# Loading the first batch in two pieces through one queue, with a new written-out order for units 0 to 2, in a fused attention and feed-forward kernel

## The chip, the cores and the metric

The kernel runs on one core of a Trainium2 chip. Times are device microseconds of one execution. Before the change the kernel takes 227.11 us (median of three executions, 226.82 to 227.4). A separate execution was profiled, and all views of the profile come from it.

Engines: PE is TensorE (matmuls and transposes; its weight loads appear as PEld), DVE is VectorE, ACT is ScalarE, POOL is GpSimd, SP is SyncE. DMAs are issued from the instruction streams of SP, ACT or POOL. Only those issued by POOL may change the number type on the way (float32 in DRAM, float16 on the chip), and each issue occupies POOL itself.

## The reference: what is computed

Attention over chunks, then a feed-forward layer. Inputs are float32: q, k, v of shape (4 batches, 8 heads, 768 tokens, 64), eight memory tokens per batch and head (mem_k, mem_v), a gain vector g of 512, and two weights of 512 x 2048 and 2048 x 512.

```python
for c in range(nc):                       # chunks of 32 tokens
    k_full = concat(mem_k, k[c_start - 16 : c_end + 8])     # clipped to the sequence
    v_full = concat(mem_v, v[c_start - 16 : c_end + 8])
    a = softmax(q_c @ k_full.T / 8)
    out_c = a @ v_full
x  = out rearranged to (batch, token, 512)
xn = (x - mean) / sqrt(var + 1e-6) * g
y  = x + relu(xn @ w_ch1) @ w_ch2
```

## The kernel before

**Tiles and units.** The 4 x 768 tokens are cut into 24 tiles of 128 tokens (six per batch) and 12 units of two tiles. For a tile `t` the steps are: `qk_products` (scores on PE), `row_max` and `less_max` on DVE, `weights` (exponential on ACT), `pt_products` and `pt_copy` (the weights transposed on PE and copied to SBUF), `val_products` (weights times V on PE), `tokens` (division by the row sum and the mean, on DVE), `shift` (mean taken off, on POOL or ACT), `x_products` and `x_copy` (transposition on PE, gain on DVE), and `square`, `root_of` (the deviation). For a unit `u` there are eight `up_products` blocks with `relu_up`, and then the second layer. Unit 0 uses `down_products` for that; from unit 1 on seven block products (`down7_products`) work on sums of blocks of the weights and of the activations (`w2_sum`, `r_sum`). `store` writes a finished tile from SP.

**Getting q, k and v into place.** Scores need K and Q with the head dimension on the partitions. `load_octets` brings rows of eight tokens ("octets", 512 numbers in a row) into `raw` with POOL's casting DMA. PE transposes them against an identity, and copies from PSUM spread the columns into `KT` (by `to_stream`, in groups of 72 columns with room for memory columns) or `QD` (by `to_rows`). `turn_whole` transposes blocks of 128 columns and needs the octets rearranged first by `mix_into`; `turn` transposes blocks of 64 columns directly from the raw rows. V of batch 0 goes the same way into `VT` (which is the buffer `KT[1]`, not yet in use), and `v_products`/`v_copy` turn it back into groups of rows in `V[0]`, group `g` by group `g` (12 groups). V of later batches is loaded directly in rows by `load_v_group` (two DMAs per group), and `v_shared` and `v_mem` copy overlapping rows and memory rows from SP.

**How batch 0 starts.** The first 16 octets of K, Q and V are loaded uncast (float32) by three DMAs on SP's queue (`load_first`, issued at L636 to L638 through L180) into `xs[6..8]`. DVE casts them to `xn` (L654, L659, L680), `first_turn` transposes them (L230), and `first_stream` and `first_rows` copy them into place. Octet 16, the right border of the first piece, comes with the memory rows in four DMAs on ACT's queue (`load_mem`, L174) and is put in place by `octet_cols`. POOL's queue brings octets 16 to 47 (`load_octets(..., 16, 32, ...)`, through L105) and then octets 48 to 95.

**What sets the order.** The schedule is manual: each engine executes its instructions in the order in which the program issues them. For units 0 to 2 that order is a list written out by hand, one call per line (L636 to L1034), including the bank of PSUM that each product uses. From unit 3 on a loop with a table of steps (`plan`) issues the work; that part and everything after it are the same in both kernels. PE, ACT, DVE, POOL and SP each wait in order, so an instruction whose data is late holds everything behind it on its engine. The casting DMAs use eight completion semaphores in turn, so the ninth issue waits until the first has landed, and so on. `warm(n, bank)` issues `n` matmuls of zeros (L633), whose results nobody reads.

Of the kernel before, what the change touches and what calls it, by code (L numbers as in the profile page):

```python
# [9 lines left out]
FP16 = mybir.dt.float16  # L10
# [6 lines left out]
def kernel(  # L17
# [12 lines left out]
    nc = tc.nc  # L30
# [16 lines left out]
    memT = sb.tile([128, B * 4 + 12, 8], FP16, name="memT")  # L47
# [8 lines left out]
    MR = B * H + 3 * H  # L56
# [121 lines left out]
    def load_first(queue, x, src):  # L178

        queue.dma_start(out=xs[6 + x], in_=dram(src, 0, [[512, 16], [HS, H], [1, 512]]))  # L180

# [30 lines left out]
    def mem_ends(dst, src, engine="V"):  # L212
# [6 lines left out]
        )  # L219

    def octet_cols(dst, src, group, engine):
        copy_on(engine)(
            out=free(dst, 16 + group * BLK, [[KC, 4], [1, 8]]), in_=free(src, 0, [[8, 4], [1, 8]]),
        )

    def first_turn(x, p):

        for r in range(8):
            for par in range(2):
                nc.tensor.matmul(  # L230
                    out=p[64 * par : 64 * par + 64, 64 * r : 64 * r + 64],
                    lhsT=xn[x][:, 64 * r : 64 * r + 64],
                    rhs=free(identity, 2 * par, [[4, 32], [1, 2]]),
                    start=True, stop=True, tile_position=(0, 64 * par),
                )
        return p

    def first_stream(dst, p, q0, n, engine):
        for first, cnt, at in ((0, 2, 16), (2, 6, 40)):
            copy_on(engine)(  # L240
                out=free(dst, q0 * KC + at, [[KC, n], [BLK, 2], [8, cnt], [1, 8]]),
                in_=free(p, q0 + 4 * first, [[1, n], [32, 2], [4, cnt], [64, 8]]),
            )

    def first_rows(p, q0, n, engine):
        copy_on(engine)(
            out=free(QD[0], q0 * S, [[S, n], [8, 16], [1, 8]]),
            in_=free(p, q0, [[1, n], [4, 16], [64, 8]]),
        )
# [386 lines left out]

    load_first(nc.sync, 0, k)
    load_first(nc.sync, 1, q)  # L638
    load_first(nc.sync, 2, v)
    load_mem(nc.scalar, 0, mem_k, B * H)  # L640
    load_mem(nc.scalar, B * H, k, H, 16 * 512, HS)
    load_mem(nc.scalar, B * H + H, mem_v, H)
    load_mem(nc.scalar, B * H + 2 * H, v, H, 16 * 512, HS)
    make_identity(nc, identity)
    nc.gpsimd.memset(V[0][:, 0:4, :, 64:VW], 1.0)
    nc.gpsimd.memset(V[0][0:16, 0, :, 64:VW], 0.0)

# [494 lines left out]
```

## Time and profile before

| What | us |
|---|---|
| median of the executions shown (lowest, highest) | 227.11 (226.82, 227.4) |
| the profiled execution | 226.66 |
| its span from first to last instruction | 224.9 |
| PE busy in the span | 215.5 |
| DVE / ACT / POOL busy | 168.4 / 129.0 / 114.7 |
| first instruction of `up_products` (the first real weights) | 23.90 |
| granted TensorE clock, mean over the span | 0.985 |

The page of the profile shows one execution. "Busy" is time in which an instruction of the engine runs; PE is busy 96% of the span, and from 25 us to the last units it is almost never idle. The chain of work that ended last is read backwards from the last instruction: each piece waits for the one before it. In the slices of the span, PEclk is the clock that was granted to TensorE, in tenths of full speed. A line number names the place in the kernel, which is often a helper's.

### The profile page before, as it was taken

The page shows a single profiled execution, that of the slowest core. Times are in us where ns is not written, and L with a number is a line of the kernel's source. Part 1 is how long each engine was busy: PE and PEld are TensorE (multiplying, and loading weights), DVE is VectorE, ACT ScalarE, POOL GpSimd, SP SyncE. Part 2 cuts the span into 40 slices and gives each one's busy share as a digit, 9 for nine tenths or more (in the row PEclk, how much of TensorE's full clock was granted, in tenths as well). Part 3 has the DMA queues.
Part 4 walks back from the last instruction along what each step waited for, and adds up shares of the span by engine and source line. Part 5 has one row for each costly group of instructions (what it writes and reads, how often), then busy time and mean ns, then how long its engine had stood idle before and what let it go on. Part 6 is the DMA issues. An engine that isn't in the chain of part 4 may idle for free.

```text
span 224.9 us, 8345 instructions
## 1 busy us (share of the span) xinstructions
PE 215.5 (96%) x3609; PEld 190.7 (85%) x3609; DVE 168.4 (75%) x382; ACT 129.0 (57%) x250; POOL 114.7 (51%) x198
## 2 busy tenths in 40 slices
PE   7879999997999999999999999999999999999993
PEld 2558985797998889999999999999999899999982
DVE  0996879986988886994786996994876876747372
ACT  2697473795896288378347198198266464443310
POOL 8899752969997817967346937321121130320000
PEclk9985999999999999999999999999999999999999
DMA  6999999999786994995934985942002002011022
GB/s 149 198 175 206 214 211 203 147 129 162 68 70 102 213 154 80 128 78 110 181 39 103 123 105 101 96 79 93 3 3 93 3 3 96 0 56 40 4 93 95
DMA packets 43530, 23.66 MB, mean 105 GB/s; under 512 B 30069, under 2 KB 39477, under 8 KB 43445
## 3 DMA queue, kind: packets, MB, share of 16 engines
q0 software_dynamic: 38032, 14.09, 54.2%
q1 hardware_dynamic: 5364, 8.93, 13.7%
q8 instruction: 28, 0.46, 0.9%
q10 hardware_dynamic: 96, 0.11, 0.2%
q14 instruction: 10, 0.07, 0.1%
HBM read 29.05 MB, written 6.29 MB: 157 GB/s over the span
## 4 chain that ended last, share of the span: by engine, by line
PE 89%; DVE 4%; ACT 2%; DMA 2%; issue 0%; POOL 0%; SPq 0%; ACTq 0%
PE upb L489 32%; PE dnb L566 28%; PE two L405 4%; PE one L306 3%; PE one L489 3%; PE dnb L489 3%; PE one L354 2%; PE one L385 2%; DMA xs<-in_q_dram 2%; PE one L461 2%; PE upb L515 2%; PE one L515 2%; PE one L566 1%; PE upb L306 1%; PE dnb L328 1%; DVE nmx L363 1%
## 5 line engine op out<-in xcount | busy, mean ns | idle before, releaser
L489 PE MATMUL upb<-xT,w1c 128*128 128x256 f16 x656 | 84.7, 273 | 0.3 <-ACT rT L481 0.3
L489 PEld LDWEIGHTS <-w1c 128*128 128x128 f16 x768 | 81.3, 114 | 2.2 <-issue 0.5
L481 ACT ACTIVATE rT<-upb 128x512 f16<-128x512 f32 x81 | 47.1, 594 | 30.0 <-PE upb L489 30.0
L573 DVE SCALAR_TENSOR_TENSOR xs<-dnb,rstd,xs 128x256 f32<-128x256 f32 x73 | 35.1, 481 | 24.1 <-PE dnb L566 23.2
L566 PEld LDWEIGHTS <-RS 128*128 128x128 f16 x352 | 33.6, 98 | 3.5 <-issue 0.2
L376 ACT ACTIVATE P<-sub 128x512 f16<-128x512 f32 x24 | 15.1, 632 | 35.1 <-DVE sub L366 35.1
L566 PE MATMUL dnb<-T,RS 128*128 128x256 f16 x248 | 31.8, 273 | 0.0
L428 POOL TENSOR_SCALAR xn<-xs,nmean 128x512 f16<-128x512 f32 x20 | 14.1, 707 | 29.2 <-PE upb L489 17.5
L566 PEld LDWEIGHTS <-rT 128*128 128x128 f16 x264 | 25.2, 98 | 2.5
L448 POOL TENSOR_SCALAR veps<-ssq 128x1 f32<-128x1 f32 x24 | 4.5, 189 | 40.7 <-ACT sq L441 40.0
L560 DVE TENSOR_TENSOR RS<-rT 128x1024 f16<-128x1024 f16 (+2 forms) x23 | 15.2, 663 | 8.9 <-ACT rT L481 8.9
L566 PE MATMUL dnb<-w2c,rT 128*128 128x256 f16 x168 | 21.6, 273 | 0.0
L441 ACT ACTIVATE sq<-xs,nmean 128x512 f16<-128x512 f32 x24 | 17.2, 718 | 0.5 <-ACT sq L441 0.4
L415 DVE CUSTOM_DVE_ANT_1 xs<-two,rec 128x512 f32<-128x512 f32 x24 | 16.6, 692 | 0.8
L452 POOL TENSOR_TENSOR rstd<-veps,mhalf 128x1 f32<-128x1 f32 x24 | 13.9, 578 | 2.0
L114 POOL DMA_DIRECT2D V<-in_v_dram x16 | 13.4, 840 | 0.7 <-PE dnb L566 0.6
L363 DVE TENSOR_REDUCE nmx<-one 128x8 f32<-128x512 f32 x19 | 13.0, 685 | 1.0 <-PE one L354 1.0
L470 DVE TENSOR_TENSOR xT<-one,g_col 128x512 f16<-128x512 f16 x16 | 11.0, 687 | 3.5 <-PE one L461 3.3
L366 DVE TENSOR_TENSOR sub<-one,nmx 128x512 f32<-128x512 f32 x19 | 13.1, 691 | 0.6
L393 ACT COPY PT<-one 128x512 f16<-128x512 f16 x16 | 9.3, 584 | 4.2 <-PE one L385 3.4
L405 PEld LDWEIGHTS <-PT 64*32 64x32 f16 x768 | 7.5, 94 | 4.9 <-issue 3.7
L566 PE MATMUL dnb<-w2c,RS 128*128 128x256 f16 x88 | 11.4, 272 | 0.0
(144 smaller groups left out, 361.3 us busy)
## 6 DMA issues: line engine op xcount, KB each, us to landing
out_dram<-xs SPq DMA_DIRECT2D x23, 256.0 KB
raw<-in_k_dram POOLq DMA_DIRECT2D x14, 192.0 KB, 6.0
raw<-in_q_dram POOLq DMA_DIRECT2D x14, 192.0 KB, 6.3
w1c<-in_moe_w_ch_dram POOLq DMA_DIRECT2D x4, 512.0 KB, 11.5
w2c<-in_moe_w_ch_dram POOLq DMA_DIRECT2D x4, 512.0 KB, 16.0
V<-in_v_dram POOLq DMA_DIRECT2D x16, 77.0 KB, 3.8
V<-memv SPq DMA_DIRECT2D x6, 120.0 KB
V<-V SPq DMA_DIRECT2D x2, 360.0 KB
```

Source lines behind the costliest of these rows:

```text
L363: nc.vector.tensor_reduce(out=nmx[t % 2], in_=scores, axis=AX.X, op=ALU.max)
L376: nc.scalar.activation(out=P[t % 3], in_=sub[t % 2], func=ACTF.Exp, scale=0.125)
L405: nc.tensor.matmul(out=two[col : col + 32, 128 * h : 128 * h + 65], lhsT=PT[t % 3][rows, 2 * (h // 4) + h % 2, q0 : q0 + 32], rhs=V[b % 2] ...
L415: nc.vector.tensor_tensor_reduce(out=x.rearrange("p (h d) -> p h d", h=H), in0=free(two, 0, [[128, 8], [1, 64]]), in1=free(r, 0, [[1, 8], ...
L428: nc.gpsimd.tensor_scalar(out=xn[i], in0=x, scalar1=m, scalar2=1.0, op0=ALU.add, op1=ALU.mult,)
L441: nc.scalar.activation(out=sq, in_=xs[t % 9], func=ACTF.Square, bias=nmean[t % 6], scale=1.0, accum_out=ssq[i],)
L452: nc.gpsimd.tensor_tensor(out=rstd[t % 9], in0=veps[i], in1=mhalf, op=ALU.pow)
L481: nc.scalar.activation(out=o, in_=i, func=ACTF.Relu)
L489: nc.tensor.matmul(out=p[:, 256 * hb : 256 * hb + 256], lhsT=free(w1c[hc // 4][:, dt, :], hc % 4, [[4, 128]]), rhs=xT[u % 3][:, dt, :], st ...
L560: nc.vector.tensor_tensor(out=RS[k][:, lo:hi, :], in0=a[:, lo:hi, :], in1=b[:, lo:hi, :], op=op)
L566: nc.tensor.matmul(out=p[:, 0:256], lhsT=left[:, n, :], rhs=right(n), start=(n == 0 and not add), stop=(n == 7), skip_group_check=add,)
L573: nc.vector.scalar_tensor_tensor(out=x, in0=p[:, 0:256], scalar=rstd[t % 9], in1=x, op0=ALU.mult, op1=ALU.add,)
```

## The change

Batch 0 is loaded only by POOL's casting queue, in a different cut: octets 0 to 47 of K and V, octets 0 to 31 of Q, then octets 32 to 95 of Q and 48 to 95 of K and V. The three uncast loads, the three casts, `first_turn`, `first_stream`, `first_rows`, `octet_cols` and the two DMAs for octet 16 are gone. K and Q of the first piece are transposed by `turn` straight from the raw rows, V by `mix_into` and `turn_whole`. The memory rows (40 instead of 56) come by two DMAs on SP's queue; the gain vector `g_col` is loaded right behind them instead of at 8.9 us. The cast of the memory rows moves from DVE to ACT, the first columns of ones in V are set by DVE instead of POOL, and `make_identity` comes on POOL behind the first three loads. The list for units 0 to 2 is another one: the same tiles and units, with other orders, banks and engines for the copies. Some of it, with the list cut where it only reorders:

```diff
-    memT = sb.tile([128, B * 4 + 12, 8], FP16, name="memT")
+    memT = sb.tile([128, B * 4 + 4, 8], FP16, name="memT")
-    MR = B * H + 3 * H
+    MR = B * H + H
-    def load_first(queue, x, src):
-        queue.dma_start(out=xs[6 + x], in_=dram(src, 0, [[512, 16], [HS, H], [1, 512]]))
-    load_first(nc.sync, 0, k)
-    load_first(nc.sync, 1, q)
-    load_first(nc.sync, 2, v)
-    load_mem(nc.scalar, 0, mem_k, B * H)
-    load_mem(nc.scalar, B * H, k, H, 16 * 512, HS)
-    load_mem(nc.scalar, B * H + H, mem_v, H)
-    load_mem(nc.scalar, B * H + 2 * H, v, H, 16 * 512, HS)
-    make_identity(nc, identity)
+    load_mem(nc.sync, 0, mem_k, B * H)
+    load_mem(nc.sync, B * H, mem_v, H)
+    nc.sync.dma_start(out=g_col, in_=dram(moe_g_ln, 0, [[1, 128], [128, 4]]))
-    warm(9, upb[0])
-    copy_on("V")(out=xn[1], in_=xs[7])
-    load_octets(0, 0, k, 0, 16, 32, (0,))
-    load_octets(0, 0, k, 0, 16, 32, (1,))
-    warm(2, one[0])
-    fq = first_turn(1, one[0])
...
+    warm(7, upb[0])
+    load_octets(0, 0, k, 0, 0, 48, (0,))
+    load_octets(0, 0, k, 0, 0, 48, (1,))
+    load_octets(1, 0, q, 0, 0, 32, (1,))
+    copy_on("A")(out=mem16, in_=mem32)
+    make_identity(nc, identity)
+    mem_products(one[0])
+    mem_copy(one[0], "V")
+    mem_cols(KT[0], memT[:, 0:4, :], "V")
+    mem_ends(KT[0], memT[:, 0:4, :], "A")
+    load_octets(1, 0, q, 0, 0, 32, (0,))
+    warm(6, one[1])
+    tk0 = turn(raw[0][0], 0, 48, one[1])
+    load_octets(2, 0, v, 0, 0, 48, (0,))
+    mem_cols(VT, memT[:, 16:20, :], "V")
+    load_octets(2, 0, v, 0, 0, 48, (1,))
+    to_stream(KT[0], tk0, 0, "V", 48, 0)
+    load_octets(1, 1, q, 0, 32, 64, (0,))
+    tk1 = turn(raw[0][0], 1, 48, upb[0])
+    to_stream(KT[0], tk1, 1, "V", 48, 0)
+    load_octets(1, 1, q, 0, 32, 64, (1,))
+    load_octets(0, 1, k, 0, 48, 48, (1,))
+    warm(1, upb[1])
+    tq1 = turn(raw[1][0], 1, 32, upb[1])
+    to_rows(0, tq1, 1, "V", 32, 0, 0, 16)
+    mix_into(whole[0], raw[2][0], 0, 96, "V")
+    load_octets(2, 1, v, 0, 48, 48, (0,))
+    load_octets(2, 1, v, 0, 48, 48, (1,))
+    tq0 = turn(raw[1][0], 0, 32, dnb[0])
+    load_octets(0, 1, k, 0, 48, 48, (0,))
+    to_rows(0, tq0, 0, "A", 32, 0, 0, 16)
+    warm(4, dnb[1])
+    s0 = qk_products(0, dnb[1])
+    tv0 = turn_whole(whole[0], 0, 96, one[0])
+    to_stream(VT, tv0, 0, "V", 48, 0)
+    load_w1(0)
+    mix_into(whole[0], raw[2][0], 1, 96, "A")
...
+    tv1 = turn_whole(whole[0], 1, 96, one[1])
+    to_stream(VT, tv1, 1, "A", 48, 0)
+    s1 = qk_products(1, upb[0])
+    row_max(1, s1)
+    warm(2, dnb[0])
+    v2 = v_products(2, dnb[0])
+    load_octets(1, 0, q, 1, 0, 48, (0,))
+    load_v_group(1, 11, 1)
+    load_w1(3)
+    v1 = v_products(1, upb[1])
+    load_w1(1)
+    mix_into(whole[3], raw[1][1], 1, 128, "A")
+    v0 = v_products(0, one[0])
+    v_copy(0, v0, "A")
+    row_max(0, s0)
+    v_copy(1, v1, "A")
+    less_max(0, s0)
+    weights(0)
+    load_octets(1, 0, q, 1, 0, 48, (1,))
+    less_max(1, s1)
...
+    load_w2(0)
+    to_rows(0, tQ1, 1, "A", 64, 32)
...
+    load_w1(2)
...
+    shift(1, "P")
+    shift(0, "A")
+    to_stream(KT[0], tK1, 1, "A", 48, 48)
+    load_w2(1)
+    warm(1, upb[1])
+    x0 = x_products(0, upb[1])
...
+    s2 = qk_products(2, dnb[1])
+    v_copy(5, v5, "V")
+    up_products(0, 1, upb[1])
...
+    shift(4, "P")
...
+    load_v_group(1, 3, 0)
...
+    v_shared(1, 0, 4)
...
+    v_mem(1)
...
+    val_products(6)
```

The list still issues 24 loads into `raw` and the weights' eight loads on POOL's queue, in another order and, for batch 0, in other sizes. `warm` issues 21 matmuls in all instead of 17. The second batch's first two Q loads stand ahead of most of the weights.

## The prediction

> **What bounds the kernel now.** I read the page's busy shares and slices first, then the chain of waits, then stages between chosen times, then the DMA issues.
>
> ```profile
> PE 215.5 (96%) x3609; PEld 190.7 (85%) x3609; DVE 168.4 (75%) x382; ACT 129.0 (57%) x250; POOL 114.7 (51%) x198
> PE   7879999997999999999999999999999999999993
> PEclk9985999999999999999999999999999999999999
> DMA  6999999999786994995934985942002002011022
> ```
>
> PE is the bound from the fourth slice (5.6 us each) on. So a change at the start counts in two ways only: when PE can begin the weights' stream, and how often PE idles afterwards. The first slices also show a cut clock. The stages (length, then busy time per engine with instructions, granted clock, DMA share, GB/s):
>
> ```profile
> 5.00:8.50 3.50, 2.73 (x56) 1.40 (x54) 2.62 (x12) 1.08 (x3) 2.75 (x5) 1.00 1.17 208
> 12.00:15.00 3.00, 2.34 (x89) 1.63 (x85) 2.82 (x7) 2.76 (x8) 2.94 (x5) 1.00 1.19 170
> 15.00:21.80 6.80, 6.13 (x110) 5.12 (x96) 4.59 (x16) 5.56 (x11) 6.41 (x11) 0.50 1.23 198
> 25.00:50.00 25.00, 25.00 (x454) 20.06 (x453) 22.41 (x50) 16.67 (x34) 14.84 (x26) 1.00 1.23 181
> 50.00:55.00 5.00, 3.80 (x96) 3.37 (x95) 2.82 (x5) 3.18 (x6) 4.94 (x8) 1.00 1.18 181
> 70.00:75.00 5.00, 4.70 (x51) 4.34 (x49) 4.37 (x9) 2.43 (x5) 4.67 (x10) 1.00 0.86 179
> 75.00:92.00 17.00, 16.79 (x296) 15.35 (x295) 13.33 (x33) 11.65 (x21) 10.17 (x18) 1.00 1.06 147
> ```
>
> Until 15 us DVE and ACT carry the work (2.82 and 2.76 of 3); from 15 to 21.8 PE runs at half clock; from 25 it is full, and idles 1.20 + 0.30 + 0.21 = 1.71 us up to 92. The chain (start, length, what) of the first 24 us:
>
> ```profile
> 1.56 4.11 DMA xs<-in_q_dram
> 5.70 0.53 DVE xn L654
> 6.27 0.77 PE one L230 x30
> ...
> 9.19 0.69 DVE nmx L363
> ...
> 15.09 0.64 ACT P L376
> ...
> 23.97 1.00 PE upb L489 x8
> ```
>
> The first useful work is at 5.70, when SP's uncast Q has landed; scores of tile 0 are ready for DVE at 9.19; the second tile's exponential starts at 15.09; the weights begin at 23.9. Issues (count, size, median us to landing):
>
> ```profile
> V<-in_v_dram POOLq DMA_DIRECT2D x16, 77.0 KB, 3.8
> raw<-in_v_dram POOLq DMA_DIRECT2D x2, 192.0 KB, 6.7
> raw<-in_k_dram POOLq DMA_DIRECT2D x2, 128.0 KB, 5.6
> ```
>
> POOL's first casting loads took 5.6 us beside the other queues, so the new start hangs on the slower way in.
>
> **The change part by part.**
>
> *K's first landing.* POOL starts its first own instruction at 0.80, so K's two pieces of 192 KB are issued at 0.80 and about 1.5 (0.55 to 0.77 per issue). Lower bound: the 77 KB row's 3.8 us plus 115 KB at 200 GB/s = 0.6, the second one piece (1.0) later: 5.8 us. Upper bound: the 192 KB row's 6.7 from 1.5: 8.2. The queue is empty then, which is nearer to the first; but the gain's 512 four-byte pieces, moved from 8.9 to the front of SP's queue, pass at the same time (without them 10 to 15 us would be nearer to 200 GB/s than to 170), for which I add 0.5. I take 6.7.
>
> *Memory rows.* Two loads on SP instead of four on ACT, without three 256 KB loads beside them: landed by about 3.5 (an estimate: Q's 256 KB took 4.11, these are 80 KB, issued at 0.8 and 1.5). ACT's table load (1.28, at 2.8 before) now waits for them, with nothing behind it that is wanted earlier; it and the cast (0.6 on ACT) end near 5.5; sixteen small transposes 0.42, to 6.0; DVE's copies (0.35, 0.5, 0.5) end at 7.4, before K is turned. Identity on POOL (0.20 + 0.29) comes 1.8 us later than before but ahead of 5.5: hidden; if K lands early it is still hidden, since the memory products stand before K on PE.
>
> *Six warm matmuls* stand between memory products and K on PE: 6 x 0.26 = 1.6 us at full clock, to 7.6; so K's landing at 6.7 is covered, and the first turn is on PE from 7.6. It costs about 0.5 (sixteen transposes of half the width, where eight of the full width take 0.34 to 0.5 in the rows of L306), so K is in PSUM at 8.2. Before, DVE started at 5.7.
>
> *DVE's list from there.* Copy of 48 octets into the stream: 0.35 + 0.75 less overlap = 1.0, twice: 10.2. Q's 16 octets 0.42: 10.6. Mix of V 0.45: 11.05. V turned on PE 0.45, copied 1.0: 12.5. Two row maxima and two subtractions, 4 x 0.69 = 2.8: 15.3. Before, the second subtraction ended at 15.06 (14.36 + 0.70). So the late start is nearly made up there, because three casts (0.5 each), the half-piece mixes and four small copies are gone: +0.25.
>
> *From there to the weights.* Before: 23.90 - 15.06 = 8.84 us. After, the list has more to do in this stretch: tile 0's transposed weights and values come behind it (0.41 copy, 1.1 for reciprocal, division and mean on DVE), and Q's 64 octets are two mixes (0.45 on DVE, 1.04 on ACT) and two copies (0.95 for 48 octets, so 1.2 on DVE and 1.0 on ACT), where before half had been done. DVE +2.0 and ACT +1.0; before, DVE idled 2.2 of the 6.8 us to 21.8 and ACT 1.2, which takes some. Bounds: 0 (all in those gaps) and 2.0. I take 1.25, in the middle, since the chain alternates between engines. Sum for the start of the weights: +0.25 + 1.25 = +1.5, at 25.4 (24.1 to 27.0).
>
> *Less left for PE.* Of the work before the weights, the new list has done one V group (0.35, the eight-transpose rows) and one 96-column turn (0.34) more; the rest of the units is the same products. -0.7.
>
> *Weights and later loads on POOL's queue.* Batch 0 is now 2304 KB there instead of 1920, but the queue starts at 0.8 rather than 2.05 and alone. At 200 GB/s it ends near 17; w1's four blocks follow at 19, 23, 25 and 31 and w2's up to 38.5 (512 KB each 2.5 us, second-batch Q 1.0 each in between). Each is wanted later: the block for the third product at 25.4 + 1.7 = 27.1, the last w1 block at about 34, w2's at 32 to 44. Hidden, by 2 us at the tightest. The ninth-issue wait costs nothing either while 2 MB are under way. POOL waits in `shift(1)` for DVE with four weight loads behind it, but the queue's backlog then reaches to 31 us.
>
> *Idle PE up to unit 3.* 1.71 before. The longest piece is PE waiting for POOL's `shift`:
>
> ```profile
> PE upb L461 <- POOL xn L428: 1.2, 1, 1.2
> ```
>
> The new list gives POOL two shifts instead of four, which may remove it; but `shift(4)` stays there, and behind it the loads of V group 3, on which the row copies and tile 6's values hang. Bounds 0 and 4.0; I take 2.0, so +0.3.
>
> *Everything from unit 3 on*: same work, PE full for 58.00 of 58 us from 92 to 150; 0.
>
> Sum: +1.5 - 0.7 + 0.3 = +1.1 us. The profiled execution took 226.66, which gives 227.76; it is 0.45 below the median of the runs, so in the median 228.2.
>
> **A rule against the change.** In the row from 15 to 21.8 the clock was 0.50, after a stage in which PE was busy 2.34 of 3 us with small transposes; nine warm matmuls took 3.82 us (0.425 each) at the beginning, and four later ones 1.04 (0.26 each). The first run of warm matmuls becomes 7 x 0.425 = 3.0 us. The Trainium skill (TensorE: Matmul & The Clock Gate, section Part 1: The HAM clock gate) says that the clock opens after about 3.4 us of sustained activity, in windows that run freely. The row of nine agrees, with 3.82; no run here shows seven. If the gate stays shut, six warm matmuls take 2.55 instead of 1.6 and two K turns 0.45 longer each: 1.9 later at the first scores.
>
> **The rivals.**
> 1. *Faster: the idle time goes.* If the new order removes all 1.71 us of idle PE up to unit 3, the sum is 1.5 - 0.7 - 1.7 = -0.9: 225.8, in the median 226.2. For it: the shift wait is one place and POOL has two shifts fewer. Against: DVE at 22.41 of 25 us has little room. It decides if the weights start before about 25.6.
> 2. *The clock stays shut longer* at the start, as above: +1.1 + 1.9, 230.1 in the median. For it: the shorter first run, then 1.3 us without work. Against: before, the gate stayed open through 12 to 15 at 2.34 of 3.
> 3. *Tile 6 waits for V.* Group 3 of the second batch is issued behind `shift(4)`, near 47 us, lands 3.8 later, then a row copy and the memory rows follow on SP (about 5 us: the 120 KB copy is in DMAs of the same size), so at 57 to 60; its values are due near 61. Two or three us late gives 230.7.
> 4. *No difference*: the extra 1.25 is hidden in DVE's and ACT's gaps, +0.25 - 0.7 + 0.3 = -0.15: 227.0.
>
> **How the numbers follow.** A measurement of this kernel tells 0.3% (0.7 us) from no change. Forecast 0.38, rival 1 0.17, rival 2 0.18, rival 3 0.12, rival 4 0.15. The forecast, 228.2, is 0.5% slower; its own range with weights between 24.7 and 26.5 is 227.5 to 229.3. The whole range leaves out less than 2 in 10 at the ends: 226.0 (most of rival 1) to 230.8 (rivals 2 and 3). Faster 0.17; same 0.15; slower 0.38 + 0.18 + 0.12 = 0.68.
>
> **What would show it.** In the profile of the changed kernel: DVE's first copy into `KT` from a bank at about 8.2 (6.7 if K comes earlier and the warm matmuls don't hold it; 10 if the clock is shut); DVE's second subtraction ending near 15.3; the first L455 (`up_products`) at 25.4; idle PE between there and 92 us near 2.0; no wait of PE or DVE on a weight's DMA. The prediction is wrong if the weights start by 24.5, if PE waits there for w1, or if tile 6 waits for V.

## The result and the profile after

The changed kernel is faster. Its median is 225.78 us (224.95 to 228.96, 16 executions) against 227.47 us (226.73 to 229.31, 16 executions) for the kernel before; the ratio is 0.9918, with a 95% interval of 0.9894 to 0.9941, so 0.8% or some 1.9 us less. The ratio leaves out one execution of the changed kernel (228.96 us), which was over 1.5% longer than the fastest of the same kernel and had a lower granted clock, 0.985. The prediction said 228.2 us, 0.5% more. The sign was wrong, and 225.78 lies below the range of 226.0 to 230.8.

The profiled execution of the changed kernel took 225.04 us (span 223.3), which is 0.74 below its median; that of the kernel before took 226.66 (span 224.9), 0.81 below its own. The two profiles, 1.62 us apart, can therefore stand for the difference of the medians (1.69).

The page of the changed kernel, busy time and the slices that the prediction showed of before:

```profile
PE 215.1 (96%) x3597; PEld 188.9 (85%) x3597; DVE 164.8 (74%) x367; ACT 130.3 (58%) x248; POOL 114.4 (51%) x195
...
PE   6987999999999999999999999999999999999994
...
PEclk9999999999999999999999999999999999999999
DMA  5999999999999994995934975942002002011022
```

PE has almost the same busy time as before (215.1 against 215.5). The cut clock in the third and fourth slices is gone, and so is the fall of the DMA engines to 7, 8 and 6 tenths in the eleventh to thirteenth slices. The stages, in the columns of the prediction (length, then busy time and instructions of PE, weight loads, DVE, ACT and POOL, granted clock, DMA share, GB/s):

```profile
5.00:8.50 3.50, 3.50 (x32) 1.53 (x34) 0.84 (x3) 0.36 (x2) 3.50 (x6) 1.00 1.23 186
12.00:15.00 3.00, 2.80 (x81) 2.09 (x80) 2.56 (x5) 2.76 (x7) 1.93 (x3) 1.00 1.24 204
15.00:21.80 6.80, 4.71 (x130) 3.57 (x126) 5.75 (x16) 6.22 (x13) 5.21 (x10) 1.00 1.28 203
25.00:50.00 25.00, 24.91 (x502) 19.41 (x500) 18.06 (x40) 18.22 (x38) 20.45 (x34) 1.00 1.20 186
50.00:55.00 5.00, 5.00 (x62) 4.97 (x60) 4.92 (x11) 4.04 (x7) 4.47 (x7) 1.00 1.17 122
70.00:75.00 5.00, 4.70 (x57) 4.12 (x58) 4.15 (x9) 2.51 (x5) 4.84 (x10) 1.00 0.85 166
75.00:92.00 17.00, 16.79 (x298) 15.57 (x298) 14.08 (x34) 11.34 (x21) 9.57 (x16) 1.00 0.95 118
```

From 15 to 21.8 us the clock is 1.00 instead of 0.50. From 25 to 50 us DVE has 18.06 us of work instead of 22.41: it is no longer close to its limit there. From 50 to 55 us PE is busy 5.00 us instead of 3.80. From 70 us on PE's busy time is that of before (4.70 and 16.79).

The timeline of the start (start, length, engine, line, operation; in brackets the idle time before it and what ended it). L599 is `warm`, L226 `turn`, L332 `less_max`, L455 `up_products` in this kernel:

```profile
1.25 3.17 PE L599 MATMUL upb<-zeros 128*128 128x512 f16 x7 [1.25 <-DVE zeros L607]
1.34 1.38 POOL L105 DMA_DIRECT2D raw<-in_k_dram  x2 [0.84 <-POOLq L1069]
...
5.45 2.74 PE L599 MATMUL one<-zeros 128*128 128x512 f16 x6
...
8.12 0.85 PE L226 MATMUL one<-identity,raw 96*64 96x96 f16 x16
...
9.01 1.02 DVE L239 COPY KT<-one 128x192 f16<-128x192 f16 x2 [2.58 <-PE one L226]
...
10.54 1.04 PE L599 MATMUL dnb<-zeros 128*128 128x512 f16 x4
...
15.27 0.68 DVE L332 TENSOR_TENSOR sub<-upb,nmx 128x512 f32<-128x512 f32 x1
...
24.27 1.94 PE L455 MATMUL upb<-xT,w1c 128*128 128x256 f16 x16
...
26.29 0.80 PEld L455 LDWEIGHTS <-w1c 128*128 128x128 f16 x8 [0.35 <-DMA w1c<-in_moe_w_ch_dram]
```

Six warm matmuls took 2.74 us, 0.46 each, so the clock was still shut; the trace's record of it has it open from 9.71 us on (four of them took 1.04 at 10.54). The second subtraction ended at 15.95, and the weights started at 24.27, only 0.37 later than before. What PE waited for between 20 and 72 us (total, times, longest), where before the longest was 1.2 us for a `shift` on POOL:

```profile
PE one L272 <- POOL T L259: 0.7, 1, 0.7
PE upb L455 <- ACT rT L447: 0.3, 1, 0.3
PE one L294 <- ACT KT L239: 0.2, 1, 0.2
```

The first and the last of these lie before the weights' start. After it PE idles 0.09 for a block of w1, 0.09 for V in tile 6, and 0.30 and 0.21 where it did so before as well: 0.69 us in all up to 92 us, against 1.71.

The account of the profiled pair. At the first product of unit 3 (71.87 before, 70.78 after) the changed kernel is 1.09 us ahead: +0.37 for the weights' start, -1.02 for idle PE behind it (1.50 before and 0.48 after, up to that point), and the rest, -0.45, put down to work that had been done by then. From there to the last matmul both take 149.3 us. Another 0.48 us is gained behind the last DVE operation, at the last store. The last DVE operation before (its span ends at 224.95) and after (at 223.33):

```profile
221.24 0.48 DVE L573 SCALAR_TENSOR_TENSOR xs<-dnb,rstd,xs 128x256 f32<-128x256 f32 x1 [0.39 <-PE dnb L566]
```

```profile
220.10 0.48 DVE L539 SCALAR_TENSOR_TENSOR xs<-dnb,rstd,xs 128x256 f32<-128x256 f32 x1 [0.39 <-PE dnb L532]
```

By the semaphores of the two traces the last store landed 2.04 us after that operation's end before and 1.75 after it now (0.29). Then SP still goes through its final waits in a fixed order, at 0.06 us each: four of them stood behind the last store's before, one stands there now (0.18).

Rows of the page on the loads of the changed kernel (count over the whole execution, size, median us to landing):

```profile
raw<-in_k_dram POOLq DMA_DIRECT2D x16, 192.0 KB, 5.8
raw<-in_q_dram POOLq DMA_DIRECT2D x12, 192.0 KB, 6.4
w1c<-in_moe_w_ch_dram POOLq DMA_DIRECT2D x4, 512.0 KB, 11.3
w2c<-in_moe_w_ch_dram POOLq DMA_DIRECT2D x4, 512.0 KB, 13.8
```

K's first two pieces landed 4.1 and 4.5 us after their issues, at 5.40 and 6.67. Counted over all landings of POOL's queue up to 39.6 us, when the last block of w2 is there, 6816 KB had landed after the change and 6208 KB before it (there by 39.2). At about 200 GB/s those 608 KB are 3 us of the queue. The weights themselves are not earlier (the last w2 block 39.6 instead of 39.2); what is earlier is the second batch's Q, both halves by 27.7 instead of 40.9. The changed list turns it on PE at 34.25 and 38.34 us, the list before at 48.69.

### The profile page after: what moved, and what is told of

Same layout as the page of the kernel before. It is cut to its first block, busy times and chain, and to the rows that moved or that the text cites. A ratio compares the mean times of both kernels' runs of the same rounds, so it can differ in the third digit from the quotient of the medians.

```text
span 223.3 us, 8291 instructions
## 1 busy us (share of the span) xinstructions
PE 215.1 (96%) x3597; PEld 188.9 (85%) x3597; DVE 164.8 (74%) x367; ACT 130.3 (58%) x248; POOL 114.4 (51%) x195
## 4 chain that ended last, share of the span: by engine, by line
PE 78%; DMA 14%; POOL 3%; DVE 1%; issue 1%; ACT 0%; SPq 0%; POOLq 0%
PE upb L455 30%; PE dnb L532 28%; DMA w1c<-in_moe_w_ch_dram 5%; PE two L371 3%; DMA raw<-in_q_dram 3%; DMA V<-memv 3%; PE one L272 3%; DMA raw<-in_k_dram 2%; PE one L320 2%; PE one L427 2%; POOL raw L105 2%; PE one L351 2%; PE dnb L455 2%; PE upb L481 2%; PE dnb L481 2%; PE one L455 1%
## 5 line engine op out<-in xcount | busy, mean ns | idle before, releaser
L455 PE MATMUL upb<-xT,w1c 128*128 128x256 f16 x656 | 84.7, 273 | 0.3 <-ACT rT L447 0.3
L455 PEld LDWEIGHTS <-w1c 128*128 128x128 f16 x768 | 81.1, 114 | 2.3 <-issue 0.5
L539 DVE SCALAR_TENSOR_TENSOR xs<-dnb,rstd,xs 128x256 f32<-128x256 f32 x75 | 36.1, 481 | 24.1 <-PE dnb L532 23.1
L532 PE MATMUL dnb<-T,RS 128*128 128x256 f16 x256 | 32.8, 273 | 0.0
L394 POOL TENSOR_SCALAR xn<-xs,nmean 128x512 f16<-128x512 f32 x18 | 12.7, 704 | 31.2 <-PE upb L455 17.5
L532 PE MATMUL dnb<-w2c,rT 128*128 128x256 f16 x176 | 22.6, 273 | 0.0
L526 DVE TENSOR_TENSOR RS<-rT 128x1024 f16<-128x1024 f16 (+2 forms) x23 | 15.3, 664 | 8.9 <-ACT rT L447 8.9
L436 DVE TENSOR_TENSOR xT<-one,g_col 128x512 f16<-128x512 f16 x18 | 12.3, 686 | 3.5 <-PE one L427 3.3
L114 POOL DMA_DIRECT2D V<-in_v_dram x16 | 13.4, 838 | 0.8 <-PE dnb L532 0.7
L359 ACT COPY PT<-one 128x512 f16<-128x512 f16 x18 | 10.5, 585 | 5.4 <-PE one L351 4.6
L239 DVE COPY KT<-one 128x192 f16<-128x192 f16 (+1 forms) x20 | 10.2, 550 | 3.4 <-PE one L226 2.6
L332 DVE TENSOR_TENSOR sub<-one,nmx 128x512 f32<-128x512 f32 x17 | 11.8, 692 | 0.6
L329 DVE TENSOR_REDUCE nmx<-one 128x8 f32<-128x512 f32 x17 | 11.7, 685 | 0.0
L532 PE MATMUL dnb<-T,rT 128*128 128x256 f16 x88 | 11.4, 273 | 0.0
## 6 DMA issues: line engine op xcount, KB each, us to landing
w2c<-in_moe_w_ch_dram POOLq DMA_DIRECT2D x4, 512.0 KB, 13.8
```

Source lines behind the costliest of these rows:

```text
L114: nc.gpsimd.dma_start(out=V[b % 2][72:128, 0 : NG - 1, h, 0:64], in_=dram(v, base + 16 * D, [[64, 56], [64 * 64, NG - 1], [1, 64]]),)
L394: nc.gpsimd.tensor_scalar(out=xn[i], in0=x, scalar1=m, scalar2=1.0, op0=ALU.add, op1=ALU.mult,)
L436: nc.vector.tensor_tensor(out=xT[(t // 2) % 3][:, :, 128 * i : 128 * i + 128], in0=pv.rearrange("p (d c) -> p d c", d=4), in1=free(g_col, ...
L455: nc.tensor.matmul(out=p[:, 256 * hb : 256 * hb + 256], lhsT=free(w1c[hc // 4][:, dt, :], hc % 4, [[4, 128]]), rhs=xT[u % 3][:, dt, :], st ...
L526: nc.vector.tensor_tensor(out=RS[k][:, lo:hi, :], in0=a[:, lo:hi, :], in1=b[:, lo:hi, :], op=op)
L532: nc.tensor.matmul(out=p[:, 0:256], lhsT=left[:, n, :], rhs=right(n), start=(n == 0 and not add), stop=(n == 7), skip_group_check=add,)
```

## The experiments

Two explanations stood against each other at the start. The first: the gain is the start, because the clock no longer closes between 15 and 21.8 us. The second: it is the middle, because PE's wait for a shift at 52 us is gone. The runs and the texts ahead of them took that shift for `shift(4)`; the trace shows that it was `shift(5)`, as told at the second run. All ratios are to the kernel before, timed on the same chip.

**The clock alone, in the kernel before.** Nine more matmuls of zeros between the small transposes:

```diff
+    warm(3, two[:, 0:512])     # ahead of v_products(0)
+    warm(2, two[:, 0:512])     # ahead of pt_products(0)
+    warm(1, two[:, 0:512])     # ahead of val_products(0)
+    warm(3, dnb[1])            # ahead of pt_products(1)
```

> The kernel before with nine more matmuls of zeros between 10 and 16 us: three ahead of v_products(0), two ahead of pt_products(0), one ahead of val_products(0), three ahead of pt_products(1), all in places where PE idled or nearly. Theory 1 (the half clock from 15.0 to 21.8 us held the kernel before back, and my sum took that stretch for work): the clock stays open, PE's 6.1 busy us there become about 3.1, the weights start at 22.4 to 23.2 instead of 23.90, and the time falls by 0.7 to 1.5 us. Theory 2 (the copies on DVE and ACT set the pace up to the weights, PE's clock is hidden behind them): the clock may open, but the weights still start at 23.7 to 24.2 and the time stays within 0.4 us.

227.46 us; ratio 1.0007 (0.9974 to 1.0041). The clock stayed open from 6.4 us on and the weights started at 23.03, 0.87 earlier than before. Nothing of that reached the end. What PE waited for between 20 and 72 us (the ACT row lies ahead of the weights' start):

```profile
PE upb L461 <- POOL xn L428: 1.5, 1, 1.5
PE upb L461 <- ACT xn L432: 0.6, 1, 0.6
PE one L515 <- DMA w2c<-in_moe_w_ch_dram: 0.6, 1, 0.6
...
PE upb L515 <- DMA w2c<-in_moe_w_ch_dram: 0.3, 1, 0.3
```

PE now waited 0.92 us for two blocks of w2 at 35 to 40 us, and 1.46 instead of 1.20 for the shift. Unit 3 began at 72.49, later than before (71.87). So the clock alone is not the gain: ahead of the loads PE can only wait for them.

The clock is not free in the old list either. Of the 98 timed executions of the kernel before that stand beside these runs, 33 had a mean granted clock of 0.980 or more and took 226.86 us in the median, 36 had 0.974 to 0.977 and took 227.23, and 29 had 0.966 to 0.970 and took 228.02. The profiled execution, at 0.985, is of the first kind: its one stretch of 6.8 us at half clock cost nothing that reached the end, as this run shows, but executions that lose more clock are up to 1.2 us longer.

**The shift alone, in the kernel before.**

```diff
-    shift(4, "P")
+    shift(4, "A")
```

> The kernel before with one word changed: shift(4) on ACT instead of POOL, so that it doesn't stand behind the DMA issues on POOL. Theory 3 (PE's 1.20 us idle at 51.5 us comes from this shift alone, and its removal is most of what the new list won after the weights' start): the idle goes, unit 3 begins 1.0 to 1.2 us earlier, time -1.0 to -1.2 us. Rival (something else is late at the same place, tile 4 or 5's chain on DVE or the V rows of tile 6): the idle shrinks to 0.5 to 1.0 us or moves, time -0.5 to 0.

227.60 us; 1.0008 (0.9976 to 1.0039). The wait is gone from the trace, the time is not. But the run moved a shift that PE did not wait for. The two shifts on POOL and their products on PE, in the kernel before:

```profile
50.11 0.70 POOL L428 TENSOR_SCALAR xn<-xs,nmean 128x512 f16<-128x512 f32 x1
...
51.13 0.39 PE L461 MATMUL dnb<-identity,xn 128*128 128x128 f16 x4
...
51.97 0.70 POOL L428 TENSOR_SCALAR xn<-xs,nmean 128x512 f16<-128x512 f32 x1
...
52.72 0.40 PE L461 MATMUL upb<-identity,xn 128*128 128x128 f16 x4 [1.20 <-POOL xn L428]
```

L428 and L461 are lines of helpers; the bank tells the tile. The list has `x4 = x_products(4, dnb[1])` and `x5 = x_products(5, upb[1])`, so the product that waited is tile 5's, and the shift that it waited for, at 51.97, is `shift(5)`. Tile 5's mean was ready at 49.99; the shift stood behind `shift(4)` and two DMA issues on POOL. In the profiled execution of this run the wait went because PE came later: the clock was at half from 13.4 to 27.0 us, the weights started at 25.53, and PE reached tile 5's product at 53.68, when `shift(5)`, still on POOL, had ended at 53.21. So this run doesn't price the wait.

**Both, in the kernel before** (the nine matmuls and `shift(4, "A")`).

> The kernel before with both edits of b_open and b_shift: nine more matmuls of zeros between 10 and 16 us, and shift(4) on ACT. Each alone changed nothing (ratios 1.0007 and 1.0008): with the clock open the weights started at 23.03 instead of 23.90, but PE then waited 1.46 us for shift(4) instead of 1.20 and 0.92 us for w2 blocks; without the wait for shift(4) that run started the weights at 25.53. Theory 4 (two limits of nearly the same length side by side, PE's own start and POOL's stream of issues up to shift(4) near 52 us; one alone is worth nothing): both together give unit 3 at 70.5 to 71.3 instead of 71.87 and a time 0.5 to 1.4 us below the kernel before. Rival (neither is a limit; something after them, w2's landing or the V rows, takes all of it): within 0.3 us of the kernel before.

226.85 us; 0.9985 (0.9963 to 1.0007): 0.3 us less, which can't be told from no change (the interval reaches to 0.8 us). The weights started at 22.78, the earliest of all, and PE then waited here:

```profile
PE upb L515 <- DMA w2c<-in_moe_w_ch_dram: 1.0, 2, 0.5
PE upb L461 <- POOL xn L428: 0.8, 1, 0.8
```

The second row is `shift(5)` again: with `shift(4)` off POOL the wait is 0.76 us instead of the 1.46 of the first run. At 84.2 us this execution idles another 0.68 for which the profile names no wait.

**One step further, in the kernel before**: both, `shift(5)` on ACT as well, and `down_products(1, 1)` (the first w2 block that was late) moved to just ahead of `(1, 2)`.

```diff
-    down_products(1, 1, upb[0])    # and put in again just ahead of (1, 2)
-    shift(5, "P")
+    shift(5, "A")
```

> b_both (the kernel before, with nine more matmuls of zeros and shift(4) on ACT) with the three waits taken away that its trace shows between the weights' start and unit 3: shift(5) goes to ACT as well (PE waited 0.76 us for it at 52.4), and the second quarter of unit 0's second layer for tile 1 moves behind scores and values that need no w2 block, to just ahead of the third (PE waited 0.55 and 0.46 us for w2 blocks at 33.3 and 36.0). Theory 4, now with three limits in a row (PE's start, w2's landing, POOL's stream up to the shifts): all 1.77 us go and with them 1.0 to 1.7 us of the time; unit 3 at 69.8 to 70.6, the time at or below the changed kernel's (ratio to before 0.988 to 0.994), though batch 0 comes in as before. Rival (the way in of batch 0 is what the changed kernel won by): the waits reappear elsewhere, time within 0.5 us of b_both's, ratio 0.996 to 1.000.

227.64 us; 1.0005 (0.9976 to 1.0035), where 0.988 to 0.994 was expected. This is the one run that takes `shift(5)` off POOL in the old list, and no gain came of it. Its profiled execution took 231.29 us, far above the median, so where the time went is not shown. These edits at the places where PE waits do not make the old list faster.

**The changed kernel without its later warm matmuls.**

```diff
-    warm(1, upb[1])
-    warm(4, dnb[1])
-    warm(2, dnb[0])
-    warm(1, upb[1])
```

> The changed kernel without its eight later matmuls of zeros (four ahead of qk_products(0), two ahead of v_products(2), one each ahead of Q's turn and of x_products(0)). Theory 1: the clock, open from 9.71 us in the changed kernel, opens later or shuts again between 12 and 23 us, and the weights start 0.7 to 2 us later than 24.27; time +0.7 to +2 us against the changed kernel (about 226.5 to 227.8 on its median's scale of 225.8). Theory 2: PE's clock is hidden behind the copies: the weights start at 24.0 to 24.5 and the time is within 0.4 us of the changed kernel's, ratio to before 0.990 to 0.994.

225.76 us; 0.9918 (0.9888 to 0.9947), the same as the changed kernel. The clock was at half only from 12.5 to 15.9 us, and the weights started at 24.00. The eight matmuls do keep the clock open in that stretch: nine of these twelve executions had a mean granted clock of 0.984 to 0.992, while 13 of the changed kernel's 16 had 0.999 or more. But the time doesn't depend on it there, and from 15.9 us on the clock was open without them.

**The changed kernel with the old first run of nine warm matmuls.**

```diff
-    warm(7, upb[0])
+    warm(9, upb[0])
-    warm(6, one[1])
+    warm(4, one[1])
```

> The changed kernel with nine matmuls of zeros first instead of seven, and four instead of six between the memory products and K's first turn. In the changed kernel the six took 2.74 us at half clock, the clock opened at 9.71, K had landed at 6.67 and its turn began at 8.12. If the run of nine opens the clock at 4.7 as it does in the kernel before, the four take 1.0, K's turn begins at 6.8 and lasts 0.5 instead of 0.85, and DVE's first copy of K starts at 7.4 instead of 9.01. Theory 1 and 2 then differ in what it is worth: if the copies set the pace, the weights start 0.6 to 1.6 us earlier (23.7 to 22.7), unless V's landing at 10.58 or w1's second block at 26.25 holds it, in which case PE idles there and the gain is 0 to 0.5. If nine don't open it either, the turn begins at 7.3 and the gain is 0 to 0.8.

225.86 us; 0.9925 (0.9893 to 0.9958). The clock opened at 6.9 instead of 9.7 us, and DVE had the first scores at 12.66 instead of 13.35. No gain came of it. The profiled execution then lost the clock from 17.1 to 24.0 us, started the weights at 25.57, and waited for V in tile 6 (row below). It is one of four of the twelve that lost clock (0.983 to 0.992, median 226.60); the other eight (0.998 or more) took 225.40 in the median, which is not clearly below the changed kernel either.

```profile
PE two L371 <- DMA V<-in_v_dram: 0.8, 1, 0.8
```

**The way in alone, under the old list.** The first 16 octets of Q, K and V by POOL's casting queue straight into `xn`; no uncast loads, no casts.

```diff
-        queue.dma_start(out=xs[6 + x], in_=dram(src, 0, [[512, 16], [HS, H], [1, 512]]))
+        queue.dma_start(out=xn[x], in_=dram(src, 0, [[512, 16], [HS, H], [1, 512]]))
-    load_first(nc.sync, 0, k)
-    load_first(nc.sync, 1, q)
-    load_first(nc.sync, 2, v)
+    load_first(nc.gpsimd, 1, q)
+    load_first(nc.gpsimd, 0, k)
...
-    copy_on("V")(out=xn[1], in_=xs[7])
+    load_first(nc.gpsimd, 2, v)
-    copy_on("V")(out=xn[0], in_=xs[6])
-    copy_on("V")(out=xn[2], in_=xs[8])
```

> The kernel before with its list, but with the first 16 octets of Q, K and V brought by POOL's casting queue straight into xn, in place of SP's uncast loads and three casts on DVE: the change's way in, without its cut and its list. Theory L (the way in matters: POOL alone lands 192 KB at 5.40, 4.1 us after its issue, in the changed kernel, against 5.67 us for 128 KB beside SP's loads): Q in xn at 5.2 to 5.8 and K at 5.9 to 6.5, so DVE's first stream copy starts within 0.5 us of the kernel before's, POOL's later pieces land 0.5 to 1.5 us later than before because 384 KB more pass there, the weights start at 23.5 to 24.6, and the time is within 0.5 us of the kernel before: the way in alone wins nothing. Rival (the way in is what won): 0.8 to 1.7 us faster than before.

229.81 us; 1.0110 (1.0076 to 1.0145), slower by 2.5 us, more than either expectation allowed. The pieces are there early (Q at 4.5, K at 5.2), but three issues more stand on POOL's queue, the first block of w1 lands at 22.1 instead of 20.6 and the last of w2 at 41.6 instead of 39.2. The weights started at 27.07. The clock may have a part in it: it was at half from 13.8 to 27.5 us, and all six executions had a mean of 0.958 to 0.970, where executions of the kernel before took 228.0 in the median. So the old list does not profit from the new way in; it loses by it, and how much of the loss is the queue's and how much the clock's isn't separated.

**The old way in, put back beside the new list.** The three uncast loads run again on SP, into buffers that nobody reads yet, and the memory rows go back to ACT's queue.

```diff
-    load_mem(nc.sync, 0, mem_k, B * H)
-    load_mem(nc.sync, B * H, mem_v, H)
+    for x, src in ((6, k), (7, q), (8, v)):
+        nc.sync.dma_start(out=xs[x], in_=dram(src, 0, [[512, 16], [HS, H], [1, 512]]))
+    load_mem(nc.scalar, 0, mem_k, B * H)
+    load_mem(nc.scalar, B * H, mem_v, H)
```

> The changed kernel with the three uncast loads of 256 KB on SP put back at the front (into buffers that nobody reads before they are overwritten) and the memory rows on ACT's queue: what sharing the way in with SP costs POOL's loads. Theory L: K's two pieces land at 7.5 to 8.5 instead of 5.40 and 6.67, K's turn starts 0 to 0.8 us later than 8.12 since the matmuls of zeros hold it until then, every later piece lands 1.5 to 2.0 us later (768 KB at 400 GB/s), w1's second block at about 28 instead of 26.25, and PE waits for it 1.5 to 2 us at 26.3; time +0.8 to +2.0 us against the changed kernel. Rival (the queues don't disturb each other): landings within 0.5 us, same time as the changed kernel, ratio to before 0.990 to 0.994.

228.92 us; 1.0062 (1.0030 to 1.0094). Against the changed kernel's 0.9918 that is 1.44%, 3.3 us, more than was expected. Its profiled execution took 230.22 us, 1.3 above its median. The stages of this run (columns as above) and the longest waits of PE up to 30 us:

```profile
5.00:8.50 3.50, 1.87 (x22) 0.88 (x22) 0.75 (x3) 1.93 (x4) 2.40 (x4) 0.89 1.14 225
12.00:15.00 3.00, 2.97 (x63) 1.40 (x58) 1.68 (x3) 1.54 (x3) 2.17 (x3) 0.57 1.21 194
```

```profile
PE one L191 <- ACT T L620: 2.2, 1, 2.2
PE one L272 <- ACT T L259: 1.6, 1, 1.6
```

K's second piece landed at 9.4 instead of 6.67, the first w1 block at 23.8 instead of 20.2 and the last w2 block at 43.5 instead of 39.6: 3.6 to 3.9 us later on the queue. The weights started at 29.17. Nobody used the 768 KB; they ran beside the casting queue, and its landings came later. Part of the delay at the start is the memory rows on ACT's queue (the 2.2 us row), which this run moves too, so the 3.3 us are not the uncast loads' alone.

**The changed kernel once more**, because its start differed from one run of these variants to the next.

> The changed kernel itself, unaltered, on the same chip as the two others, to compare them with: 0.990 to 0.994 of the kernel before.

225.27 us (224.77 to 226.29); 0.9909 (0.9880 to 0.9938). Its profiled execution took 226.29 us, 1.25 more than the first one of the same program, and the timeline shows why:

```profile
5.39 2.74 PE L599 MATMUL one<-zeros 128*128 128x512 f16 x6
...
11.02 1.89 PE L599 MATMUL dnb<-zeros 128*128 128x512 f16 x4
...
25.60 1.61 PE L455 MATMUL upb<-xT,w1c 128*128 128x256 f16 x13
```

The four warm matmuls at 11 us took 1.89 us instead of 1.04: here the clock opened only at 14.06. The weights started 1.33 us later, and the execution ended 1.25 us later. In the changed kernel this later start passed through to the end. Six profiled executions of this kernel and its near variants agree (weights' start, then the whole time): 24.00 and 225.26 (without later warm matmuls), 24.27 and 225.04, 24.61 and 224.72 (the next run); 25.57 and 226.72 (nine first), 25.60 and 226.29, 25.88 and 226.17 (the last run). The means of the three early ones and of the three late ones differ by 1.39 in the start and 1.39 in the time; within each three, where the programs differ, the order of the starts is not that of the times. In the old list it was not so: 23.03 gave 227.46, 22.78 gave 227.07, 23.90 gave 226.66.

**Three attempts at a better version.** First: nine warm matmuls first, w1's second and fourth blocks ahead of the second batch's loads, and the memory rows loaded 13 us and copied (`v_mem`) 11 us earlier.

```diff
-    load_octets(1, 0, q, 1, 0, 48, (0,))
-    load_v_group(1, 11, 1)
+    load_w1(1)
...
-    load_w1(1)
+    load_octets(1, 0, q, 1, 0, 48, (0,))
+    load_v_group(1, 11, 1)
...
+    nc.gpsimd.memset(memv16[:, :, :, 64:VW], 1.0)
+    load_mem_rows(1, B)
...
+    v_mem(1)
```

> The changed kernel with nine and four matmuls of zeros instead of seven and six, w1's second and fourth blocks ahead of the second batch's first Q load and V rows on POOL's queue, and the second batch's memory rows loaded and copied (load_mem_rows, v_mem) some 15 us earlier, since tile 6's values waited for V's memory copy at 60.3 in the changed kernel (0.09) and at 62.0 when the start was moved (0.79). If the start and these two are the limits that are left, the weights start at 22.8 to 23.8, w1's second block lands before it is wanted, tile 6 doesn't wait and the time is 0.5 to 1.3 us below the changed kernel's (ratio to before 0.986 to 0.990). If w2's landings or the clock take it, the time is within 0.4 us of the changed kernel's.

229.43 us; 1.0074 (1.0037 to 1.0111), slower. The timeline (issue on SP; DVE's rearranging of Q; PE's next product):

```profile
42.12 1.59 SPq L156 DMA_DIRECT2D V<-memv  x2
...
52.89 0.76 DVE L259 COPY raw<-raw 96x1024 f16<-96x1024 f16 x2 [6.06 <-DMA raw<-in_q_dram]
...
54.30 1.03 PE L455 MATMUL one<-xT,w1c 128*128 128x256 f16 x8 [3.48 <-DVE xT L436]
```

The copies of the memory rows, 120 KB each, landed at 46.7 and 49.9. POOL's loads beside them came late: a group of V issued at 43.0 landed at 49.7, and Q landed at 52.9 (48.4 in the changed kernel). That the copies held them back is read from these times; the run also moves w1's loads. DVE stood 6.06 us in front of that Q, and behind it on DVE was the `xT` that PE needed.

Second: nine warm matmuls first, w1's second block ahead of its fourth, and `v_mem` one step earlier, ahead of `v_shared`.

```diff
-    load_w1(3)
-    v1 = v_products(1, upb[1])
     load_w1(1)
+    v1 = v_products(1, upb[1])
+    load_w1(3)
...
+    v_mem(1)                   # ahead of v_shared(1, 0, 4)
...
-    v_mem(1)
```

> The changed kernel with nine and four matmuls of zeros instead of seven and six, w1's second block issued ahead of its fourth, and the memory copy into V (v_mem) issued on SP ahead of the row copy (v_shared), without loading anything earlier. The run that only moved the start (nine and four) was the same as the changed kernel, with 0.79 us of waiting for V at 62.0. If V's copies are the limit that then held it, they land at 55 to 58 instead of 60.3, tile 6 doesn't wait, and the earlier start shows: 0.3 to 1.0 us below the changed kernel (ratio to before 0.987 to 0.990). If the clock or another wait takes it, within 0.3 us of the changed kernel.

225.02 us (224.72 to 226.81); 0.9906 (0.9870 to 0.9942). The waits for w1 and for V are gone and unit 3 begins at 70.50. Beside the changed kernel's 225.27 in the same comparison that is 0.25 us, and the intervals overlap: not shown to be better.

Third: the second with `mix_into(whole[3], raw[1][1], 1, 128, "A")` and the turn behind it moved later, since in the second PE had waited 1.88 us for them at 15.6 us.

```diff
-    mix_into(whole[3], raw[1][1], 1, 128, "A")   # put in again behind weights(1)
-    tQ1 = turn_whole(whole[3], 1, 128, one[1])   # put in again behind pt_copy(0)
```

> a_next (the changed kernel with nine and four matmuls of zeros, w1's second block ahead of its fourth, v_mem ahead of v_shared) with the mix of Q's second half for one head group and its turn moved behind the two exponentials on ACT and behind the first transposed weights on PE. In a_next K's turn began at 6.7 instead of 8.1, but the weights still started at 24.61: ACT waited with that mix for Q's piece landing at 14.5, held the exponentials behind it, and PE idled 1.88 us at 15.6. If that wait is what holds the start, it goes, the weights start at 22.8 to 24.0, and since nothing else waited in a_next up to unit 3 (0.30 us idle), the time falls by as much: 0.5 to 1.5 us below a_next (ratio to before 0.984 to 0.989). If POOL's stream or V's copies take it, within 0.3 us of a_next.

226.03 us (224.30 to 228.37); 0.9919 (0.9891 to 0.9947). No gain: the one wait became four between 14.7 and 22.6 us (0.68, 0.61, 1.10, 0.50), and the clock was at half from 17.75 to 21.17.

## Why the prediction was wrong

By its steps; times are of the profiled execution.

| Step | predicted | measured |
|---|---|---|
| K's second piece landed | 6.7 | 6.67 |
| DVE's first copy of K | 8.2 (10 if the clock is shut) | 9.01 |
| second subtraction ends | 15.3 | 15.95 |
| from there to the weights | 8.84 + 1.25 = 10.1 | 8.32 |
| weights start | 25.4 | 24.27 |
| less left for PE | -0.7 | -0.45 |
| idle PE from the weights to 92 us | 2.0 | 0.69 |
| unit 3 to the last matmul | no change | -0.06 |
| from there to the end | no change | -0.48 |

**The first failed step is "from there to the weights".** The prediction took the 8.84 us of before as the fixed part and put 1.25 us of new work on it. But some 6.8 of those 8.84 us ran at half clock, as its own row from 15 to 21.8 us showed (0.50), and it never asked whether the new list would keep that. With the clock open the old list needs 7.48 us for the same stretch (both runs with nine more warm matmuls). So the half clock was worth 1.37 us of the stretch (of the weights' start 0.87 and 1.12, since in those two runs the second subtraction ended 0.5 and 0.25 later), and the new work costs 8.32 - 7.48 = 0.84, inside the bounds of 0 and 2.0 and near the 1.25 taken. The other executions of the new list bear this out in part: it needed 7.83 to 8.57 us in four executions with an open clock and 10.3 in the two variants that lost it in this stretch; but the second of the three attempts needed 9.31 with an open clock, because PE waited 1.88 us there behind ACT's mix of a late piece of Q. The step's term for the new work was about right, and its base held the half clock.

**The second failed step is "idle PE up to unit 3".** The 2.0 us was a middle between 0 and 4; 0.48 up to unit 3's first product, 0.69 up to 92 us, was measured. The prediction saw that two shifts fewer on POOL might remove the wait, but kept it because `shift(4)` stays there in the new list. That was a misreading: PE had waited for `shift(5)`, and the new list gives `shift(5)` to ACT. Tile 5's mean is ready at 50.84 there, the shift starts at once, and its product waits for nothing:

```profile
51.00 0.71 ACT L398 ACTIVATE xn<-xs,nmean 128x512 f16<-128x512 f32 x1
...
52.05 0.39 PE L427 MATMUL dnb<-identity,xn 128*128 128x128 f16 x4
```

The 1.02 us of idle time won up to unit 3 are this wait (1.20) less the two new ones (0.09 each). Rival 1 is nearest to what happened, since most of the idle time went. That its price is near as well (226.2 in the median against 225.78) is partly luck: its sum was +1.5 - 0.7 - 1.7, and +0.37 - 0.45 - 1.02 was measured, with 0.48 at the end that it didn't have. The argument against it, DVE at 22.41 of 25 us, described the old list: DVE has 18.06 us there now.

Together these are 1.13 us at the weights' start and 1.32 us of idle time; the work done earlier was 0.25 us less than forecast. That is 2.20 us, from +1.1 to -1.1 at unit 3.

**A third step was put at nothing: the end.** The sum took everything from unit 3 on as unchanged, and 0.48 us were gained behind the last DVE operation. The traces separate two parts. The last store landed 2.02 to 2.19 us after that operation in the six profiled kernels with uncast loads on SP's queue, and 1.72 to 1.78 in the eight without. And the order of SP's final waits, which differs from kernel to kernel, added 0.24 us behind that landing before and 0.06 after. Why loads of the first microseconds go with a later landing at the end is not shown.

**What was right.** K's landing came within 0.03 us; it holds 0.5 us for the gain's small pieces that no run separates, so part of that closeness may be luck. The warning about seven warm matmuls was right as well: they took 3.17 us and did not open the clock, so six more ran at 0.46 us each, and K came out of PSUM 0.8 us late. This is rival 2's mechanism, at a smaller price: 0.65 us at the second subtraction in this execution. In the repeated execution, with the clock shut until 14.06, the start and the end are 1.3 us later, against the 1.9 us that rival 2 named. The Trainium skill (TensorE: Matmul & The Clock Gate, section Part 1: The HAM clock gate) says that the clock opens after one busy window of about 3.4 us, and that the windows run freely, so that the moment varies from run to run. The trace agrees that the moment varies: the same program opened it at 9.71 and at 14.06 us, and a first run of nine opened it at 4.7 us in one execution and not before its end at 5.3 in another. The two openings of the same program lie 4.35 us apart, which is more than one such window, so the place of the window alone doesn't explain them. The wait of tile 6 for V was real and tiny, 0.09 us (0.40 in the repeated execution), so rival 3 had the place right and the price wrong. PE's wait for a block of w1, 0.09 us, is also one that the text said would not be there: the margin of 2 us at the tightest was gone, since the block landed at 26.25 and PE had come to it at 26.2.

**Why the gain is there at all.** In the profiled pair the 1.62 us are mainly the wait for `shift(5)` (1.20), the end (0.48) and the work already done when the weights start (0.45), less the later start (0.37) and the two new waits (0.18). With the clock open the old list gains nothing, because PE then meets the loads of w2. In the profiled executions the old list's first products on the four blocks of w2 begin 2.19, 0.63, 0.10 and 0.32 us after the block has landed; with nine more matmuls it is 1.57, 0.04, 0.04 and 0.04, so no room is left, and PE stood 0.92 us in front of two of them. The changed list uses them 1.57, 2.00, 1.88 and 4.21 us after their landing, although the last of them lands 0.4 us later: its order has room there. Also shown: loading the first octets by the casting queue costs 1.1% under the old list, and the new list loses 1.4% when the uncast loads run beside it and the memory rows come by ACT's queue. Argued, not shown: that the room in the new list comes of its second-batch Q, which is there 13 us earlier and gives PE other work while w2 lands. Open as well: why the old list gained nothing when the clock, both shifts and one block of w2 were changed together (1.0005). How much of the gain is the list's alone can't be told, since it is written for the new cut and doesn't run with the old one.

## What to carry to other kernels

Before a measured stretch is used as a base to add to, read its granted clock: a stretch at half clock holds time that a new order can win back or lose without any change in its work. A wait is named by the line of a helper; before moving the operation, find by the bank or the time which call it was: here the wrong shift was argued about and moved. Where several limits end at nearly the same time, removing one wait may win nothing; ask what the engine would meet next, and by how much. When a DMA queue is busy over the whole start, count what other queues move beside it as a delay of everything on it: here 768 KB went with 3.6 to 3.9 us.

## What the runs showed that was not expected

- Uncast loads of 768 KB on SP's queue, which nobody waited for, went with landings on POOL's casting queue that were 3.6 to 3.9 us later (the run moves the memory rows to ACT's queue too). That is as long as 768 KB of the casting queue's own output takes at the 200 GB/s of these rows (3.9 us); the expectation had put the cost of these loads at 0.8 to 2.0 us.
- The clock can close in the same stretch of work in one execution and stay open in another. Over 15 to 21.8 us the changed kernel kept 1.00 with PE busy 4.71 of 6.8 us; variants of it lost the clock at 12.5, 17.1 or 17.75 us for 3.4 or 6.8 us, and with nine matmuls first four of twelve executions of one program lost it and eight did not. What decides it is not settled.
- In the first 10 us the column of the granted clock says 1.00 while matmuls of 512 columns take 0.43 to 0.46 us each, against 0.26 later; the record of the clock begins only with its first opening. The duration of a known matmul tells more there than the column.
- Two copies of 120 KB within the chip took 4.5 and 6.3 us (issued at 53.1 and 53.9, landed at 57.6 and 60.3), and in the run that issued them 11 us earlier the second half of Q landed at 52.9 instead of 48.4.
